# Reciprocal roots of a layer norm on GpSimd, two token tiles at a time, and normalising spread among later work

## The chip, the cores and the metric

The kernel runs on one core of a Trainium2 chip. A core has a matrix engine (TensorE, "PE" in the profile, with its weight loads as "PEld"), a vector engine (VectorE, "DVE"), a scalar engine (ScalarE, "ACT"), a general engine (GpSimd, "POOL") and an engine that issues transfers (SyncE, "SP"). Each runs its own instructions in order; between engines, semaphores say when data is ready. The metric is the device time of one execution in microseconds.

## The reference

Two stages follow each other. The first is attention with a sliding window of 128 positions and 4 sink positions, for 4 batches, 8 heads, 768 positions and 64 values a head. The second is a gated MLP over the 512 joined values of a position:

```python
h = gelu(x @ w_in)                      # 512 -> 1024
u, v = h[..., :512], h[..., 512:]
mu  = mean(v, axis=-1); var = mean((v - mu) ** 2, axis=-1)
v_n = (v - mu) / sqrt(var + 1e-06) * g_ln
v_s = einsum('ts,bsd->btd', w_sg, v_n) + b_sg[None, :, None]
out = x + (u * v_s) @ w_out
```

The mean and the variance are taken per position over 512 values. The product with w_sg mixes all 768 positions, so its first result needs the normalised values of every position of the batch.

## The kernel before, in words

The order of the instructions is written out by hand (manual_schedule): each engine does its work in the order in which the Python code issues it.

Attention runs over 16 pairs of heads (four pairs a batch). For a pair n, GpSimd casts q and k to bf16 (repack, issued two pairs ahead), TensorE transposes them, computes scores (score), ScalarE takes exponentials, VectorE multiplies by the band mask (keep_band), and TensorE multiplies by v (values); VectorE then divides by the sum of the row (L315, L316) and so writes x. GpSimd also copies the four sink keys (L214) and issues the loads of v and of the weights; SP issues the loads of q and k, the transposes of x and the output stores.

The MLP of a batch b, called a block here, is worked on when the first pair of the next batch has its scores (n = 4, 8, 12), and once more after the last pair. The function hidden(b, between) issues it:

- hidden_v for each of six token tiles j of 128 positions: four matmuls into PSUM (hv), Gelu on ScalarE into v_all (L335), bn_stats (L337) and bn_aggr (L338) on VectorE, which leave mean and variance in mv. After tiles 0 and 1 some of the values steps of the next batch are put in between (the list "between").
- hidden_u eight times: four matmuls (hu) and Gelu into uT (L348).
- inverse_root, issued after the first hidden_u: VectorE computes the reciprocal root of all six variances of a position at once, on tiles of 128x6: it adds 1e-6 (L357), makes a first guess by an integer shift and a subtraction on the bits (L358, L360), and takes three Newton steps of three instructions each (L364, L366, L367). That is 12 instructions.
- normalise, six times, one after each of the next hidden_u: VectorE subtracts the mean and multiplies by the reciprocal root, v_all to vn, 128x512 (L373).

What follows is put into a list of fillers: spatial (six matmuls over the six token tiles of vn, L383, then two VectorE instructions, L386 and L389, of which the first reads b_bc and g_sb) eight times, and project (L397) six times. For batch 0 the list begins with six transposes of w_sg (spatial_weights: wps on TensorE, wsgT on VectorE, L182). The main loop spreads the fillers among the attention steps of the next batch; for the last block there is no attention left, and they run one after the other. The tag "mm" in PSUM, which hv, hu, wps, vs and o_ps share, has two buffers.

Of the kernel before, what the change touches and what calls it, by code (L numbers as in the profile page):

```python
# [8 lines left out]
F32 = mybir.dt.float32  # L9
BF16 = mybir.dt.bfloat16  # L10
AF = mybir.ActivationFunctionType
ALU = mybir.AluOpType
# [5 lines left out]
def kernel(  # L18
# [14 lines left out]
    nc = tc.nc  # L33
# [7 lines left out]
    NT = S // 128  # L41
# [11 lines left out]
    small = ctx.enter_context(tc.tile_pool(name="small", bufs=4))  # L53
# [123 lines left out]
    def spatial_weights(si):  # L177
        wps = ps_m.tile([128, NT, 128], BF16, name="wps", tag="mm")
        for ti in range(NT):
            nc.tensor.transpose(wps[:, ti, :],  # L180
                                wsg_sb[:, ti, 128 * si:128 * (si + 1)], iden)
        nc.vector.tensor_copy(wsgT[:, si, :], wps.rearrange("p t q -> p (t q)"))  # L182
# [142 lines left out]
    uTs, vns, gTs, v_alls, mvs, rstds = {}, {}, {}, {}, {}, {}  # L325

    def hidden_v(b, j):
        if j == 0:
            v_alls[b] = work.tile([128, NT, DF], F32, name="v_all", tag="v_all", bufs=1)
            mvs[b] = small.tile([128, NT, 2], F32, name="mv", bufs=2)  # L330
        h_ps = ps_m.tile([128, 512], F32, name="hv", tag="mm")
        for c in range(KD):
            nc.tensor.matmul(h_ps, xT[b][:, c, 128 * j:128 * (j + 1)],  # L333
                             w_in_sb[:, c, DF:], start=(c == 0), stop=(c == KD - 1))
        nc.scalar.activation(out=v_alls[b][:, j, :], in_=h_ps, func=AF.Gelu_apprx_tanh)  # L335
        st = small.tile([128, 6], F32, name="st")
        nc.vector.bn_stats(out=st, in_=v_alls[b][:, j, :])  # L337
        nc.vector.bn_aggr(out=mvs[b][:, j, :], in_=st)  # L338

    def hidden_u(b, f, n):  # L340
        if f == 0 and n == 0:
            uTs[b] = work.tile([128, KU, S], BF16, name="uT")
        h_ps = ps_m.tile([128, 512], F32, name="hu", tag="mm")
        for c in range(KD):
            nc.tensor.matmul(h_ps[:, 0:NH], w_in_sb[:, c, 128 * f:128 * (f + 1)],  # L345
                             xT[b][:, c, NH * n:NH * (n + 1)],
                             start=(c == 0), stop=(c == KD - 1))
        nc.scalar.activation(out=uTs[b][:, f, NH * n:NH * (n + 1)],  # L348
                             in_=h_ps[:, 0:NH], func=AF.Gelu_apprx_tanh)

    I32 = mybir.dt.int32

    def inverse_root(b):
        rstd = rstds[b] = small.tile([128, NT], F32, name="rstd", bufs=2)
        var = small.tile([128, NT], F32, name="var", bufs=2)
        tmp = small.tile([128, NT], F32, name="tmp", bufs=2)
        nc.vector.tensor_scalar_add(var, mvs[b][:, :, 1], 1e-6)  # L357
        nc.vector.tensor_single_scalar(tmp.bitcast(I32), var.bitcast(I32), 1,  # L358
                                       op=ALU.logical_shift_right)
        nc.vector.tensor_scalar(out=rstd.bitcast(I32), in0=tmp.bitcast(I32),  # L360
                                scalar1=-1.0, scalar2=float(0x5F3759DF),
                                op0=ALU.mult, op1=ALU.add)
        for _ in range(3):
            nc.vector.scalar_tensor_tensor(out=tmp, in0=rstd, scalar=-0.5, in1=rstd,  # L364
                                           op0=ALU.mult, op1=ALU.mult)
            nc.vector.tensor_mul(tmp, tmp, var)  # L366
            nc.vector.scalar_tensor_tensor(out=rstd, in0=tmp, scalar=1.5, in1=rstd,  # L367
                                           op0=ALU.add, op1=ALU.mult)

    def normalise(b, j):  # L370
        if j == 0:
            vns[b] = work.tile([128, NT, DF], BF16, name="vn")
        nc.vector.tensor_scalar(out=vns[b][:, j, :], in0=v_alls[b][:, j, :],  # L373
                                scalar1=mvs[b][:, j, 0:1], scalar2=rstds[b][:, j:j + 1],
                                op0=ALU.subtract, op1=ALU.mult)

    def spatial(b, f, n):
        if f == 0 and n == 0:
            gTs[b] = work.tile([128, KU, S], BF16, name="gT")
        cols = slice(NH * n, NH * (n + 1))  # L380
        vs = ps_m.tile([128, 512], F32, name="vs", tag="mm")
        for si in range(NT):
            nc.tensor.matmul(vs[:, 0:NH], vns[b][:, si, 128 * f:128 * (f + 1)],  # L383
                             wsgT[:, si, cols], start=(si == 0), stop=(si == NT - 1))
        gv = small.tile([128, NH], BF16, name="gv")
        nc.vector.scalar_tensor_tensor(  # L386
            out=gv, in0=vs[:, 0:NH], scalar=g_sb[:, f:f + 1], in1=b_bc[:, cols],
            op0=ALU.mult, op1=ALU.add)
        nc.vector.tensor_mul(gTs[b][:, f, cols], gv, uTs[b][:, f, cols])  # L389

    def project(b, t, queue=nc.sync, by=nc.vector, cols=slice(0, DM)):
        rows = slice(128 * t, 128 * (t + 1))
        o_ps = ps_m.tile([128, 512], F32, name="o_ps", tag="mm")[:, 0:cols.stop - cols.start]
        whole = by is nc.vector
        res = x_sb[b][:, cols.start // 128:cols.stop // 128, t, :]
        for c in range(KU):
            nc.tensor.matmul(o_ps, gTs[b][:, c, rows], w_out_sb[:, c, cols],  # L397
                             start=(c == 0), stop=(c == KU - 1 and whole))
        if whole:
            o_sb = small.tile([128, DM], F32, name="o_sb", bufs=6)  # L400
            nc.vector.tensor_add(  # L401
                o_sb[:, cols].rearrange("p (h d) -> p h d", d=128),
                o_ps.rearrange("p (h d) -> p h d", d=128), res)
        else:
            nc.tensor.matmul(o_ps.rearrange("p (h d) -> p h d", d=128), iden, res,
                             start=False, stop=True)
            o_sb = small.tile([128, DM], F32, name="o_act", bufs=3)
            nc.scalar.copy(o_sb[:, cols], o_ps)
        queue.dma_start(out=out[b, rows, cols], in_=o_sb[:, cols])

    def project_halves(b, t, queue):
        project(b, t, queue, nc.scalar, slice(DM // 2, DM))
        project(b, t, queue, nc.vector, slice(0, DM // 2))
# [8 lines left out]
    def hidden(b, between, queue=nc.sync):  # L422
        def step():
            if between:
                between.pop(0)()

        for j in range(NT):
            hidden_v(b, j)
            for _ in range(min(j + 1, 2)):
                step()  # L430
        for i in range(2 * KU):
            hidden_u(b, i % KU, i // KU)
            if i == 0:
                inverse_root(b)
            elif i <= NT:
                normalise(b, i - 1)
        if b == 0 and queue is nc.sync:
            fillers.extend(lambda si=si: spatial_weights(si) for si in range(NT))
        for n in range(2):
            for f in range(KU):  # L440
                fillers.append(lambda f=f, n=n: spatial(b, f, n))
        for t in range(NT):
            if b == B - 1 and t == NT - 1:
                fillers.append(lambda t=t: project_halves(b, t, queue))
            else:
                by = nc.scalar if b == B - 2 else nc.vector
                fillers.append(lambda t=t, by=by: project(b, t, queue, by))
# [104 lines left out]
    def stable_path():  # L552
        keep, push = stable_masks()
        for b in range(B):
            for hp in range(HP):
                stable_pair(HP * b + hp, keep, push)
            hidden(b, [], nc.gpsimd)
            fill(len(fillers))
# [12 lines left out]
    for n in range(NP):  # L571
# [44 lines left out]
        if n % HP == 0 and n > 0:  # L616
            fill(len(fillers))
            hidden(n // HP - 1, [lambda i=i: values(n, i) for i in range(HT)])
            half_valued = n
# [10 lines left out]
    compare_inverses()  # L630
    fill(1)
    hidden(B - 1, [])
    fill(2)
    for eng in (nc.tensor, nc.vector, nc.scalar, nc.gpsimd):
# [43 lines left out]
```

## Time and profile before

| | |
|---|---|
| median of 3 runs | 180.08 us (179.92 to 180.32) |
| the profiled execution | 180.66 us |
| its span, first to last instruction | 178.80 us |
| busy: TensorE / VectorE / ScalarE / GpSimd | 156.6 / 146.0 / 119.4 / 57.5 us |
| L373 normalise, 24 instructions | 11.3 us, 543 ns each |
| L364, L366, L367 Newton steps, 12 instructions each | 2.0 us each line, 166 ns each |
| GpSimd, 128x768 cast of q or k (L191) | 823 ns (k), 826 ns (q, median) |
| GpSimd, 64x4 copy of the sink keys (L214) | 185 ns median, 180 to 376 |

How to read it: the profile is one execution. A line of a group names the source line, the engine, the operation, the tiles written and read and the number of instructions; after the bar stand the busy time in us, the mean duration in ns, and the idle time of the engine just before those instructions with what ended it. A line of a timeline has the start in us from the beginning of the span, the duration in us, the engine, the line and the tiles, and in brackets the idle time ahead of it; equal instructions that follow each other are drawn together (x6). The "chain that ended last" follows the execution back from its last instruction, at each step to what released it.

### The profile page before, as it was taken

The numbers are of one execution on the slowest core, as the hardware profiler recorded it, in microseconds if no ns is written. First come the engines' busy times: TensorE is split into PE (matmuls) and PEld (weight loads), VectorE is DVE, ScalarE is ACT, GpSimd is POOL, SyncE is SP. The second block draws the span as 40 slices with busy tenths as digits, with TensorE's granted clock in tenths as the row PEclk, the third lists the DMA queues.
The fourth block names the chain that finished last, engine by engine and source line by source line (L and its number), as shares of the span: only waits on it lengthen the run. The fifth ranks groups of instructions, "written<-read, shape, count | busy, mean of one in ns | idle before, by whom it ended". The sixth has DMA issues, their size and how long they took to land.

```text
span 178.8 us, 3744 instructions
## 1 busy us (share of the span) xinstructions
PE 156.6 (88%) x1407; PEld 88.7 (50%) x1418; DVE 146.0 (82%) x359; ACT 119.4 (67%) x168; POOL 57.5 (32%) x98
## 2 busy tenths in 40 slices
PE   0769779799689999899899999899799999999970
PEld 0447556345556555445456545355465554555430
DVE  5665989599889999698999998699999948858950
ACT  2488999867938668666968668877986856640000
POOL 8459999950042060425006070550010000000000
PEclk9999999999999999999999999999999999999999
DMA  5999999999857739895285969986202241011072
GB/s 158 266 306 265 267 271 273 191 207 218 103 179 48 202 66 209 303 270 39 20 219 33 214 183 192 380 108 44 44 4 44 50 178 59 0 63 60 0 294 66
DMA packets 47974, 27.24 MB, mean 152 GB/s; under 512 B 33680, under 2 KB 44944, under 8 KB 47952
## 3 DMA queue, kind: packets, MB, share of 16 engines
q0 software_dynamic: 27904, 6.31, 37.5%
q1 hardware_dynamic: 19504, 20.26, 37.5%
q10 hardware_dynamic: 544, 0.39, 0.7%
q8 instruction: 12, 0.20, 0.5%
q14 instruction: 10, 0.08, 0.1%
HBM read 24.81 MB, written 6.29 MB: 174 GB/s over the span
## 4 chain that ended last, share of the span: by engine, by line
PE 75%; ACT 12%; issue 4%; DVE 4%; DMA 2%
PE vs L383 17%; PE hu L345 13%; PE o_ps L397 11%; PE hv L333 11%; ACT ex L264 7%; PE sc L260 7%; PE cps L197 5%; PE av L305 4%; ACT kT L204 3%; PE scs L275 2%; PE av L308 2%; DMA k_sb<-in_k_dram 2%; ACT qT L204 2%; PE av L311 1%; DVE ex L271 1%
## 5 line engine op out<-in xcount | busy, mean ns | idle before, releaser
L264 ACT ACTIVATE ex<-sc 128x1024 bf16<-128x1024 f32 (+1 forms) x48 | 45.6, 958 | 16.9 <-PE sc L260 16.7
L383 PE MATMUL vs<-wsgT,vn 128*128 128x384 bf16 x192 | 35.5, 327 | 0.5 <-DVE wsgT L182 0.4
L191 POOL CAST k_bf<-k_sb 128x768 bf16<-128x768 f32 x15 | 12.3, 823 | 42.7 <-DMA k_sb<-in_k_dram 31.8
L397 PE MATMUL o_ps<-w_out_sb,gT 128*128 128x512 bf16 (+1 forms) x93 | 23.8, 370 | 1.2 <-DVE o_sb L401 0.8
L271 DVE TENSOR_TENSOR ex<-ex,mask 128x1024 bf16<-128x1024 bf16 x32 | 23.0, 722 | 1.8 <-ACT ex L264 1.7
L333 PE MATMUL hv<-w_in_sb,xT 128*128 128x512 bf16 x92 | 22.2, 379 | 1.9 <-DVE xT L286 1.7
L383 PEld LDWEIGHTS <-vn 128*128 128x128 bf16 x192 | 17.9, 98 | 12.0 <-issue 1.2
L345 PE MATMUL hu<-xT,w_in_sb 128*128 128x384 bf16 x128 | 23.2, 325 | 0.1
L260 PE MATMUL sc<-qT,kT 64*128 64x256 bf16 x192 | 19.0, 280 | 2.2 <-DVE qT L240 1.3
L386 DVE SCALAR_TENSOR_TENSOR gv<-vs,g_sb,b_bc 128x384 bf16<-128x384 f32 x32 | 19.5, 611 | 1.7 <-PE vs L383 1.7
L348 ACT ACTIVATE uT<-hu 128x384 bf16<-128x384 f32 x32 | 15.7, 490 | 6.5 <-PE hu L345 6.3
L337 DVE BATCH_NORM_STATS2 st<-v_all 128x6 f32<-128x512 f32 x24 | 16.3, 677 | 4.6 <-ACT v_all L335 4.5
L335 ACT ACTIVATE v_all<-hv 128x512 f32<-128x512 f32 x24 | 14.3, 597 | 7.2 <-PE hv L333 6.9
L316 DVE TENSOR_TENSOR x<-av,inverses 128x384 bf16<-128x384 f32 x32 | 17.8, 557 | 1.1
L305 PE MATMUL av<-v_sb,ex 128*128 128x65 bf16 x192 | 18.2, 198 | 0.2 <-DVE x L316 0.2
L305 PEld LDWEIGHTS <-ex 128*128 128x128 bf16 x192 | 14.5, 100 | 7.2 <-issue 2.9
L345 PEld LDWEIGHTS <-w_in_sb 128*128 128x128 bf16 x128 | 12.4, 97 | 10.7 <-issue 2.9
L87 POOL DMA_DIRECT2D v_sb<-in_v_dram x16 | 16.6, 1036 | 0.0
L308 PE MATMUL av<-v_sb,ex 128*128 128x65 bf16 x160 | 16.5, 197 | 0.0
L214 POOL COPY sk<-kT 64x4 bf16<-64x4 bf16 x30 | 6.2, 207 | 28.2 <-ACT kT L204 27.3
L191 POOL CAST q_bf<-q_sb 128x768 bf16<-128x768 f32 x15 | 14.1, 938 | 3.0 <-DMA q_sb<-in_q_dram 2.2
L333 PEld LDWEIGHTS <-xT 128*128 128x128 bf16 x96 | 9.0, 98 | 11.9 <-DVE xT L286 2.6
(83 smaller groups left out, 241.4 us busy)
## 6 DMA issues: line engine op xcount, KB each, us to landing
k_sb<-in_k_dram SPq DMA_DIRECT2D x15, 384.0 KB, 5.5
q_sb<-in_q_dram SPq DMA_DIRECT2D x15, 384.0 KB, 6.1
out_dram<-o_sb SPq DMA_DIRECT2D x17, 256.0 KB, 3.5
v_sb<-in_v_dram POOLq DMA_DIRECT2D x16, 192.0 KB, 6.9
out_dram<-o_act SPq DMA_DIRECT2D x6, 256.0 KB, 2.0
wsg_sb<-in_moe_w_sg_dram POOLq DMA_DIRECT2D x2, 576.0 KB, 10.2
w_in_sb<-in_moe_w_in_dram POOLq DMA_DIRECT2D x4, 256.0 KB, 8.9
w_out_sb<-in_moe_w_out_dram POOLq DMA_DIRECT2D x1, 512.0 KB, 11.8
```

Of the source, the lines that this page charges most:

```text
L191: eng.tensor_copy(flat.rearrange("p t (h d) -> p h t d", h=2), src)
L260: nc.tensor.matmul(sc[:, hl, w:w + n_q], kT[rows, 128 * j:128 * (j + 1)], qT[rows, 128 * j:128 * j + n_q], start=True, stop=True)
L264: nc.scalar.activation(out=part, in_=sc[:, :, 0:w], func=AF.Exp, scale=scale)
L271: nc.vector.tensor_mul(part, part, m)
L305: nc.tensor.matmul(av[:, m, hl, :], probs(i, hl, 0), v_sb[:, hl, i, :], start=(m == 0 and hl == 0), stop=False)
L308: nc.tensor.matmul(av[:, m, hl, :], probs(i - 1, hl, 1), v_sb[:, hl, i - 1, :], start=False, stop=False)
L316: nc.vector.tensor_mul(x_sb[b][:, hp, HT * c:HT * (c + 1), :].rearrange("p i (h d) -> p i h d", h=2), av[:, :, :, 0:64], rcp.to_broadcast( ...
L333: nc.tensor.matmul(h_ps, xT[b][:, c, 128 * j:128 * (j + 1)], w_in_sb[:, c, DF:], start=(c == 0), stop=(c == KD - 1))
L345: nc.tensor.matmul(h_ps[:, 0:NH], w_in_sb[:, c, 128 * f:128 * (f + 1)], xT[b][:, c, NH * n:NH * (n + 1)], start=(c == 0), stop=(c == KD - 1))
L383: nc.tensor.matmul(vs[:, 0:NH], vns[b][:, si, 128 * f:128 * (f + 1)], wsgT[:, si, cols], start=(si == 0), stop=(si == NT - 1))
L386: nc.vector.scalar_tensor_tensor(out=gv, in0=vs[:, 0:NH], scalar=g_sb[:, f:f + 1], in1=b_bc[:, cols], op0=ALU.mult, op1=ALU.add)
L397: nc.tensor.matmul(o_ps, gTs[b][:, c, rows], w_out_sb[:, c, cols], start=(c == 0), stop=(c == KU - 1 and whole))
```

## The change

The reciprocal roots are made by GpSimd instead of VectorE, in three groups of two token tiles (128x2), each issued as soon as the statistics of its two tiles are issued. The seed no longer needs a shift: one instruction multiplies the bits as an integer by -0.5 and adds the constant. A Newton step is four GpSimd instructions instead of three on VectorE, so a group has 14 instructions. The normalising of tile 0 is issued after the statistics of tile 3, that of tile 1 after those of tile 4, that of tile 2 after those of tile 5, and the other three after the first three hidden_u. The tiles var and tmp have four buffers instead of two.

```diff
-    def inverse_root(b):
-        rstd = rstds[b] = small.tile([128, NT], F32, name="rstd", bufs=2)
-        var = small.tile([128, NT], F32, name="var", bufs=2)
-        tmp = small.tile([128, NT], F32, name="tmp", bufs=2)
-        nc.vector.tensor_scalar_add(var, mvs[b][:, :, 1], 1e-6)
-        nc.vector.tensor_single_scalar(tmp.bitcast(I32), var.bitcast(I32), 1,
-                                       op=ALU.logical_shift_right)
-        nc.vector.tensor_scalar(out=rstd.bitcast(I32), in0=tmp.bitcast(I32),
-                                scalar1=-1.0, scalar2=float(0x5F3759DF),
+    def inverse_root(b, j):
+        if j == 0:
+            rstds[b] = small.tile([128, NT], F32, name="rstd", bufs=2)
+        rstd = rstds[b][:, j:j + 2]
+        var = small.tile([128, 2], F32, name="var")
+        tmp = small.tile([128, 2], F32, name="tmp")
+        nc.gpsimd.tensor_scalar_add(var, mvs[b][:, j:j + 2, 1], 1e-6)
+        nc.gpsimd.tensor_scalar(out=rstd.bitcast(I32), in0=var.bitcast(I32),
+                                scalar1=-0.5, scalar2=float(0x5F3759DF),
                                 op0=ALU.mult, op1=ALU.add)
         for _ in range(3):
-            nc.vector.scalar_tensor_tensor(out=tmp, in0=rstd, scalar=-0.5, in1=rstd,
-                                           op0=ALU.mult, op1=ALU.mult)
-            nc.vector.tensor_mul(tmp, tmp, var)
-            nc.vector.scalar_tensor_tensor(out=rstd, in0=tmp, scalar=1.5, in1=rstd,
-                                           op0=ALU.add, op1=ALU.mult)
+            nc.gpsimd.tensor_mul(tmp, rstd, rstd)
+            nc.gpsimd.tensor_mul(tmp, tmp, var)
+            nc.gpsimd.tensor_scalar(out=tmp, in0=tmp, scalar1=-0.5, scalar2=1.5,
+                                    op0=ALU.mult, op1=ALU.add)
+            nc.gpsimd.tensor_mul(rstd, tmp, rstd)
...
         for j in range(NT):
             hidden_v(b, j)
+            if j % 2 == 1:
+                inverse_root(b, j - 1)
             for _ in range(min(j + 1, 2)):
                 step()
+            if j >= 3:
+                normalise(b, j - 3)
         for i in range(2 * KU):
             hidden_u(b, i % KU, i // KU)
-            if i == 0:
-                inverse_root(b)
-            elif i <= NT:
-                normalise(b, i - 1)
+            if i < NT - 3:
+                normalise(b, i + 3)
```

In the compiled order of GpSimd the 42 instructions of block 0 stand ahead of the casts of pair 7, of its v load and of the loads of b_bc, g_sb and w_out; those of blocks 1 and 2 stand ahead of the casts and the v load of pairs 11 and 15. Each of the 42 waits for the one before it.

## The prediction

> **What bounds the kernel now.** I first read the page's chain that ended last, then the groups, then the instructions of VectorE in time order around the edited code.
>
> ```profile
> PE 156.6 (88%) x1407; PEld 88.7 (50%) x1418; DVE 146.0 (82%) x359; ACT 119.4 (67%) x168; POOL 57.5 (32%) x98
> PE 75%; ACT 12%; issue 4%; DVE 4%; DMA 2%
> L383 PE MATMUL vs<-wsgT,vn 128*128 128x384 bf16 x192 | 35.5, 327 | 0.5 <-DVE wsgT L182 0.4
> L383 PEld LDWEIGHTS <-vn 128*128 128x128 bf16 x192 | 17.9, 98 | 12.0 <-issue 1.2 <-DVE vn L373 0.9
> ```
>
> TensorE carries 75% of the chain, VectorE 4%. The edited code feeds TensorE through vn alone, and TensorE's weight loads waited 0.9 us for it in all. So at most about that can be won directly at vn; what can be lost is whatever vn becomes late by. In the last block nothing else is left for TensorE to do, and its row of VectorE shows how late vn may be:
>
> ```profile
> 148.74 0.69 DVE L337 BATCH_NORM_STATS2 st<-v_all 128x6 f32<-128x512 f32 x1
> 149.47 0.18 DVE L338 BATCH_NORM_AGGREGATE mv<-st 128x2 f32<-128x6 f32 x1
> ...
> 152.92 0.18 DVE L338 BATCH_NORM_AGGREGATE mv<-st 128x2 f32<-128x6 f32 x1
> 153.14 0.17 DVE L357 TENSOR_SCALAR var<-mv 128x6 f32<-128x6 f32 x1
> 153.34 0.17 DVE L358 TENSOR_SCALAR tmp<-var 128x6 int32<-128x6 int32 x1
> ...
> 155.56 2.83 DVE L373 TENSOR_SCALAR vn<-v_all,mv,rstd 128x512 bf16<-128x512 f32 x6
> ```
>
> ```profile
> 159.37 7.97 PE L383 MATMUL vs<-wsgT,vn 128*128 128x384 bf16 x48
> ```
>
> vn is complete at 158.39 and the spatial products begin at 159.37; the sixth of them, the first to need the last token tile, starts 5 x 0.165 later at 160.2. Slack: 1.8 us. Two rows price GpSimd and its sharing with VectorE:
>
> ```profile
> 5.46 0.42 POOL L244 COPY sk<-kT 64x4 bf16<-64x4 bf16 x2 [0.78 <-ACT kT L238]
> ```
>
> ```profile
> 82.05 1.01 POOL L87 DMA_DIRECT2D v_sb<-in_v_dram  x1
> ```
>
> ```profile
> 82.38 0.66 DVE L360 TENSOR_SCALAR rstd<-tmp 128x6 int32<-128x6 int32 x1
> ```
>
> The pair of tiny copies, the second of which waits for the first, takes 0.42 us at 0.18 each: a dependent step is 0.24. And L360, 0.17 us when alone, lasted 0.66 and ended at 83.04 with the GpSimd instruction beside it (83.06).
>
> **The change, part by part.**
>
> *Removed from VectorE:* 12 instructions a block, from 153.14 to 155.56, 2.4 us, four times. Off TensorE's path except through vn, so worth nothing unless vn comes earlier.
>
> *Added on GpSimd:* three groups of 14 dependent instructions a block (one add, one seed, three times four), 42 steps in a row. Price p of a step: from above the 128x128 affine selects on GpSimd (0.29) plus the 0.06 hand-over seen in the pair, 0.35; from below the 128x1 memset (0.10, reads nothing) plus 0.06, 0.16. The nearest row is the tiny copy, 0.24, but nine of the fourteen read two operands, so I go a quarter of the way up: p = 0.27, a group 3.8 us, three groups 11.3 us. They cannot overlap: GpSimd runs in order and each starts where the one before ended.
>
> *The wait that this adds:* normalise of tile 0 now stands on VectorE behind the statistics of tile 3 and waits for group 0; behind it are queued the statistics of tiles 4 and 5, on which group 2 depends. Walk for the last block: statistics of tile 1 end at 149.65, group 0 runs 149.75 to 153.5; normalise 0, statistics 4, normalise 1, statistics 5 (0.47, 0.8, 0.47, 0.8) end at 156.1, inside group 1; tiles 2 and 3 follow group 1, tiles 4 and 5 group 2, another 1.0.
>
> *Contention:* the four normalisings beside groups 1 and 2 and GpSimd's instructions hold each other up, as L360 shows. Bounds per normalising: 0, and its whole 0.54. I take 0.4 (its pace, 2.83/6 = 0.47, less the hand-over gap), C = 1.6 us a block (0 to 2.2). [...]
>
> So vn is complete S + 42p + C + 1.0 = S + 13.9 us, where S is 0.1 after the statistics of tile 1. Each block has a time D up to which that costs nothing:
>
> - Block 0: S = 36.0, so 49.9. VectorE's next work came at 45.01 with 0.77 idle behind it, D = 45.8: reciprocal, mask multiplies and the six wsgT copies all lie behind normalise, and TensorE's first spatial product waited for a wsgT copy. +4.1.
> - Block 1: S = 77.75, 91.7. vn ended at 87.71 with TensorE already waiting; only the 0.67 that it then idled for the kT copy absorbs anything, D = 88.4. +3.3.
> - Block 2: S = 116.1, 130.0. vn 125.71 plus an idle 0.93, D = 126.6. +3.4.
> - Block 3: S = 149.75, 163.7, D = 160.1. +3.6, nothing behind it to hide in.
>
> Sum 14.4 us. After blocks 0 to 2 TensorE is the chain again, so I take nothing back.
>
> *What GpSimd queues behind the groups:* casts of a later pair, its v load, the sk copies. In block 1 the casts of pair 11 move from 80.3 to about 90, and TensorE transposes them from 93.7 (then also later): covered. In block 2 the casts of pair 15 move from 117.4 to about 128.5 against 131.2: covered, with 1 us to spare and TensorE late as well. SP's loads into the freed buffers were waiting behind the transposes and output stores on SP's queue anyway (long waits of L321 and L409 there), so they do not move by this. In block 0 more is queued: casts and v load of pair 7, then b_bc, g_sb and w_out, issued at 36.0 to 38.1 before. Group 2 ends at 48.9; casts 1.8 and v load 1.04 put b_bc at 51.7. It took 10.6 us to land then, behind two 576 KB loads in the same queue; the k_sb loads of the same 384 KB take 5.2 (median). By 5.2 it lands at 57, g_sb a little later; gv, now due at 56.2, must end before the third spatial unit at 58.3 (two PSUM buffers). I take +1.0 (0 to 4.7).
>
> *Moved on VectorE:* six normalisings, the same count and form, costed in the walk.
>
> Total +15.4. The profiled execution took 180.66 us (span 178.80), the median of the runs is 180.08; 180.66 + 15.4 = 196.1, against the median **195.5 us**.
>
> **Rivals.**
>
> 1. *The step is dear where two operands are read.* Nine at 0.35 and five at 0.24 make a group 4.35 us: delays of 5.8, 5.0, 5.2 and 5.3, with b_bc 22.3, **202.4 us**; all at 0.35, +29, **209 us**. For it: nothing in the trace shows GpSimd with two inputs. Against: these are two elements a partition, and the affine selects' 0.29 has 128 in it. [...]
> 2. *b_bc lands late in block 0:* at 10.6 us gv ends at 63.0, TensorE loses 4.7 instead of 1.0, **199 us**. For: the only row of that load. Against: the large loads ahead of it are gone by then.
> 3. *No contention and the copy's 0.24:* delays of 1.2, 0.4, 0.5 and 0.7, **183 us**. For: the gaps between GpSimd's steps may be enough for a normalising. Against: L360.
> 4. *The other side: the groups finish in time and VectorE gains.* Place: the deadlines D above; D minus S is 9.8 to 10.6, so with C = 1.6 it decides at p = 0.17 to 0.19. With p = 0.16 and C = 0, vn is complete 7.7 after S, 0.9 to 2.3 us sooner than before, and the waits for vn (0.9) and wsgT (0.8) go: 180.08 - 1.7 = **178.4 us**; with C = 1.6 it ends near 180. For: memsets of 0.10. Against: they read nothing, and every GpSimd instruction that reads SBUF here lasts at least 0.18.
>
> **How the numbers follow.** Forecast (p 0.22 to 0.31, 186 to 203): 0.62. Rival 1: 0.14. Rival 2: 0.06. Rival 3: 0.08. Rival 4: 0.10, of it 0.06 faster and 0.04 no difference (0.2% is about what a measurement of this kernel can tell). Faster 0.06, same 0.04, slower 0.90. The range goes from rival 3 to the upper end of rival 1: 183.5 to 209; the forecast's own is 186 to 203.
>
> **What the changed profile would show.** L373 no longer six in a row but with VectorE idle before tiles 0, 2 and 4, released by GpSimd's rstd (by the walk about 2.1, 2.0 and 3.7 us in the last block). GpSimd's groups 3.8 us long, back to back, longer where a normalising lies in them. TensorE's weight load at L383 waiting for vn three to five us in each of blocks 1 to 3 and for wsgT in block 0. What makes me wrong: steps under 0.19 us, or GpSimd starting a dependent step without the 0.06 hand-over.

## The result, and the profile after

The changed kernel took **202.1 us** (median of 4 runs, 201.2 to 204.0) against 180.2 us for the kernel before on the same chip (179.9 to 180.7). The ratio is **1.120**, 95% interval 1.115 to 1.125: 12% slower. The profiled execution took 201.21 us with a span of 199.4, against 180.66 and 178.8, so the two profiles differ by 20.6 us of span. The forecast was 195.5 us with a range of 183.5 to 209. The direction and the range held; 6.6 us were missing. Each ratio below is to the kernel before on the same chip and leaves out executions more than 1.5% above the fastest of their kernel; the profiled executions of experiment 1, of the kernel with two Newton steps (5) and of the early loads alone (7) are such slow ones.

The page of the changed kernel: the busy line and the row of TensorE's granted clock (PEclk, in tenths, 40 equal slices), the chain that ended last, and the groups around the edit.

```profile
PE 164.1 (82%) x1407; PEld 90.7 (45%) x1418; DVE 140.4 (70%) x311; ACT 119.4 (60%) x168; POOL 93.6 (47%) x266
PEclk9999999999589999999789999998599999996996
PE 36%; POOL 26%; DVE 12%; issue 10%; DMA 9%; ACT 4%; ACTq 0%; POOLq 0%; DVEq 0%
L383 PE MATMUL vs<-wsgT,vn 128*128 128x384 bf16 x192 | 41.1, 355 | 11.2 <-DVE vn L373 10.6
L373 DVE TENSOR_SCALAR vn<-v_all,mv,rstd 128x512 bf16<-128x512 f32 x24 | 15.2, 660 | 26.6 <-POOL rstd L368 26.6
L383 PEld LDWEIGHTS <-vn 128*128 128x128 bf16 x192 | 19.1, 105 | 26.9 <-DVE vn L373 13.1
```

GpSimd has gone into the chain with 26%, TensorE has fallen from 75% to 36%. (Most of the 9% of DMA are loads at the start of the kernel, up to 12.9 us, and the load of g_sb in block 0.) VectorE stands idle for 26.6 us in front of its normalisings (0.1 before), TensorE's matmuls and weight loads stand idle behind vn. And the clock row is no longer all nines: there is a dip in each block (the last slice lies at the end of the work). The 192 spatial matmuls are the same, but take 355 ns each instead of 327.

The last block, GpSimd in time order (start, duration, engine and line; the idle time ahead in brackets):

```profile
165.88 0.21 POOL L359 TENSOR_SCALAR var<-mv 128x2 f32<-128x2 f32 x1 [16.81 <-DVE mv L338]
166.18 0.19 POOL L360 TENSOR_SCALAR rstd<-var 128x2 int32<-128x2 int32 x1
166.45 0.19 POOL L364 TENSOR_TENSOR tmp<-rstd 128x2 f32<-128x2 f32 x1
166.72 0.20 POOL L365 TENSOR_TENSOR tmp<-tmp,var 128x2 f32<-128x2 f32 x1
167.00 0.19 POOL L366 TENSOR_SCALAR tmp<-tmp 128x2 f32<-128x2 f32 x1
...
169.76 0.21 POOL L359 TENSOR_SCALAR var<-mv 128x2 f32<-128x2 f32 x1
...
173.84 0.21 POOL L359 TENSOR_SCALAR var<-mv 128x2 f32<-128x2 f32 x1
...
174.47 0.38 POOL L364 TENSOR_TENSOR tmp<-rstd 128x2 f32<-128x2 f32 x1
```

A step lasts 0.19 to 0.21 and the next one starts 0.27 to 0.30 after it starts, whether it reads one operand or two. The first group takes 3.88 us (165.88 to 169.76), the second 4.08; in it and in the third a few steps are longer, 0.38 at most, where a normalising runs on VectorE. VectorE and TensorE in the same block:

```profile
169.71 0.55 DVE L373 TENSOR_SCALAR vn<-v_all,mv,rstd 128x512 bf16<-128x512 f32 x1 [2.27 <-POOL rstd L368]
...
173.79 1.00 DVE L373 TENSOR_SCALAR vn<-v_all,mv,rstd 128x512 bf16<-128x512 f32 x2 [1.47 <-POOL rstd L368]
177.92 1.00 DVE L373 TENSOR_SCALAR vn<-v_all,mv,rstd 128x512 bf16<-128x512 f32 x2 [3.12 <-POOL rstd L368]
```

```profile
175.44 0.82 PE L383 MATMUL vs<-wsgT,vn 128*128 128x384 bf16 x4
178.52 5.72 PE L383 MATMUL vs<-wsgT,vn 128*128 128x384 bf16 x22 [2.25 <-DVE vn L373]
```

VectorE waits before tiles 0, 2 and 4, as the walk said. vn is complete at 178.92. TensorE does four products with the tiles that are there, then stands for 2.25 us. Twenty-two products in 5.72 us are 0.26 each; before the change 48 took 7.97, 0.166 each. Most of that is the clock. These are windows of the changed kernel: for three of its slow stretches the 3.4 us ahead, then the stretch. The columns are the busy time of each engine with the number of instructions, then the granted clock (PEclk), the share of the DMA engines and GB/s:

```profile
175.84:179.24 3.40, 1.03 (x6) 0.34 (x5) 1.06 (x3) 0.24 (x1) 1.46 (x8) 1.00 0.41 154
179.24:182.68 3.44, 3.44 (x13) 1.60 (x12) 1.96 (x4) 0.00 (x0) 0.00 (x0) 0.50 0.01 2
93.94:97.35 3.41, 0.69 (x4) 0.28 (x6) 2.35 (x4) 0.21 (x1) 3.16 (x7) 1.00 0.01 2
97.35:100.76 3.41, 3.41 (x20) 1.51 (x19) 2.58 (x6) 1.71 (x2) 1.10 (x3) 0.50 1.16 108
134.90:138.30 3.40, 1.12 (x8) 0.25 (x4) 0.96 (x2) 2.36 (x3) 2.50 (x12) 1.00 0.00 0
138.30:145.10 6.80, 4.60 (x23) 1.85 (x24) 5.13 (x9) 1.71 (x2) 3.98 (x8) 0.50 0.62 51
```

TensorE was busy for 1.03, 0.69 and 1.12 us of 3.4 at the full clock (30%, 20% and 33%); then the granted clock is 0.50 for 3.4 us, or twice that. The wait for vn is thus paid twice: while it lasts, and in the work right behind it, where six spatial products take 2.12 us (at 98.38, block 1) instead of 1.14.

The profiles of all the runs together say more. In each of them the changes of the granted clock lie multiples of 3.41 us apart (in the changed kernel's it halves at 49.55, 97.34, 138.30 and 179.26 us and is whole again at 56.38, 100.75, 145.13 and 182.67). Cut into windows at these marks, the 14 profiles have 29 windows at full clock in which TensorE's matmuls were busy for 45% or less, and half clock follows every one of them; it follows none of the 625 windows above 57%, and 5 of the 17 between. At half clock, windows of 78% or less were followed by half clock again, those of 88% or more by full clock. So in these profiles half clock goes with the share of a window in which TensorE works, and the change lies between 45% and 57%. The marks lie at other times in each profile (in block 0 half clock begins at 49.55 us in the changed kernel's, at 51.4 in the one-group kernel's of experiment 2). In the kernel with two Newton steps (experiment 5) TensorE was busy for 1.33 us of the 3.41 from 46.69 us on, 39%, and yet the twelve spatial products behind it took 2.11 us, their time at full clock. So it seems to matter how a wait lies to the marks, which no run shows by itself.

Where the 20.6 us lie, from the first matmul of one block's hv to the next block's (the fourth: to the end of the span; us):

| | block 0 | block 1 | block 2 | block 3 |
|---|---|---|---|---|
| before | 43.09 | 37.56 | 34.51 | 32.63 |
| after | 48.66 | 42.42 | 40.61 | 37.16 |
| longer by | 5.57 | 4.86 | 6.10 | 4.53 |
| predicted | 5.1 (4.1 and 1.0) | 3.3 | 3.4 | 3.6 |

The first stage starts 0.46 us earlier in this execution, which is the rest. So the delays came in the right blocks, and those of blocks 1 to 3 were sized 0.9 to 2.7 us too small in the forecast. The experiments ask what that remainder is, and which part of the change costs the rest.

### The profile page after: what moved, and what is told of

It is laid out like the page before. It is cut to its first block, busy times and chain, and to the rows that moved or that the text cites. A ratio compares the mean times of both kernels' runs of the same rounds, so it can differ in the third digit from the quotient of the medians.

```text
span 199.4 us, 3868 instructions
## 1 busy us (share of the span) xinstructions
PE 164.1 (82%) x1407; PEld 90.7 (45%) x1418; DVE 140.4 (70%) x311; ACT 119.4 (60%) x168; POOL 93.6 (47%) x266
## 4 chain that ended last, share of the span: by engine, by line
PE 36%; POOL 26%; DVE 12%; issue 10%; DMA 9%; ACT 4%; ACTq 0%; POOLq 0%; DVEq 0%
PE vs L383 12%; PE o_ps L397 9%; DMA q_sb<-in_q_dram 6%; PE sc L260 4%; POOL tmp L364 4%; POOL rstd L368 4%; POOL tmp L365 4%; POOL tmp L366 4%; DMA g_sb<-in_moe_g_ln_dram 3%; PE cps L197 3%; DVE gv L386 3%; DVE vn L373 2%; PE av L305 2%; POOL q_bf L191 2%; PE hv L333 2%
## 5 line engine op out<-in xcount | busy, mean ns | idle before, releaser
L383 PE MATMUL vs<-wsgT,vn 128*128 128x384 bf16 x192 | 41.1, 355 | 11.2 <-DVE vn L373 10.6
L373 DVE TENSOR_SCALAR vn<-v_all,mv,rstd 128x512 bf16<-128x512 f32 x24 | 15.2, 660 | 26.6 <-POOL rstd L368 26.6
L383 PEld LDWEIGHTS <-vn 128*128 128x128 bf16 x192 | 19.1, 105 | 26.9 <-DVE vn L373 13.1
L191 POOL CAST k_bf<-k_sb 128x768 bf16<-128x768 f32 x15 | 13.4, 896 | 37.8 <-DMA k_sb<-in_k_dram 33.3
L271 DVE TENSOR_TENSOR ex<-ex,mask 128x1024 bf16<-128x1024 bf16 x32 | 23.6, 739 | 0.7 <-ACT ex L264 0.7
L260 PE MATMUL sc<-qT,kT 64*128 64x256 bf16 x192 | 19.6, 289 | 2.2 <-DVE qT L240 1.3
L337 DVE BATCH_NORM_STATS2 st<-v_all 128x6 f32<-128x512 f32 x24 | 16.4, 683 | 4.6 <-ACT v_all L335 4.5
L305 PE MATMUL av<-v_sb,ex 128*128 128x65 bf16 x192 | 17.8, 196 | 0.5 <-DVE x L316 0.5
L308 PE MATMUL av<-v_sb,ex 128*128 128x65 bf16 x160 | 16.1, 195 | 0.0
L408 ACT COPY o_act<-o_ps 128x512 f32<-128x512 f32 (+1 forms) x7 | 3.7, 549 | 20.3 <-PE o_ps L405 20.3
L191 POOL CAST q_bf<-q_sb 128x768 bf16<-128x768 f32 x15 | 13.5, 899 | 5.0 <-DMA q_sb<-in_q_dram 3.2
```

Source lines behind the costliest of these rows:

```text
L191: eng.tensor_copy(flat.rearrange("p t (h d) -> p h t d", h=2), src)
L260: nc.tensor.matmul(sc[:, hl, w:w + n_q], kT[rows, 128 * j:128 * (j + 1)], qT[rows, 128 * j:128 * j + n_q], start=True, stop=True)
L271: nc.vector.tensor_mul(part, part, m)
L305: nc.tensor.matmul(av[:, m, hl, :], probs(i, hl, 0), v_sb[:, hl, i, :], start=(m == 0 and hl == 0), stop=False)
```

## The experiments

**1. Is the clock a cost of its own?** The changed kernel, with matmuls that nobody reads where TensorE would wait: ahead of the third transposes of w_sg in block 0, and ahead of the first spatial products in blocks 1 to 3.

```diff
+    def keep_busy(ps, count):
+        for _ in range(count):
+            nc.tensor.matmul(ps, w_in_sb[:, 0, 0:128], w_in_sb[:, 0, 0:384],
+                             start=True, stop=True)
     def spatial_weights(si):
+        if si == 2:
+            keep_busy(ps_t.tile([128, 384], F32, name="busy", tag="tp"), 18)
...
+        if b > 0 and f == 0 and n == 0:
+            keep_busy(vs[:, 0:NH], 14 if b == B - 1 else 22)
```

> The changed kernel with idle matmuls put where TensorE waits (18 between the second and the third transposition of w_sg in block 0, 22 ahead of the first spatial product in blocks 1 and 2, 14 in block 3; each overwritten or never read). GpSimd and VectorE are untouched. Theory A (the waits for vn cost about 15 us, and the rest of the 22 us is TensorE's granted clock, which reads 0.5 for some microseconds after each long wait): the clock stays near 1.00 and the time falls to 196 us (194 to 199). Theory B (the half clock lies beside other engines' work and costs nothing; the waits alone make the 22 us): 201 to 203 us, whatever the clock reads.

Measured: 197.73 us (196.9 to 199.9), ratio 1.0944 [1.0892, 1.0997]. The idle matmuls made the kernel 4.4 us faster than without them (ratio 1.094 instead of 1.120). In the profiled execution (199.9 us, the slowest of the four) block 1 went from 42.42 to 41.18 and the last from 37.16 to 35.64; block 2 still had a stretch at half clock (143.0 to 146.4) and was longer (41.65 against 40.61), as its group 0 started 2.2 us after the statistics of tile 1 (0.95 without the idle matmuls); block 0 was no shorter (48.83), and VectorE waited there 1.90 us for g_sb (1.53 in the changed kernel):

```profile
57.15 0.62 DVE L395 SCALAR_TENSOR_TENSOR gv<-vs,g_sb,b_bc 128x384 bf16<-128x384 f32 x1 [1.90 <-DMA g_sb<-in_moe_g_ln_dram]
```

Theory A held: with the clock at 0.982 to 0.998 instead of 0.934 to 0.948 the time is inside its 194 to 199. The clock is a term that the forecast did not have.

**2. Is it the engine or the three groups?** Two kernels undo one half of the change each. The first keeps GpSimd, but takes all six variances at once, with the normalisings where they were before:

```diff
-            if j % 2 == 1:
-                inverse_root(b, j - 1)
-            if j >= 3:
-                normalise(b, j - 3)
...
-            if i < NT - 3:
-                normalise(b, i + 3)
+            if i == 0:
+                inverse_root(b)
+            elif i <= NT:
+                normalise(b, i - 1)
```

> Only the engine is changed: GpSimd computes all six roots in one group of 14 steps, at the place of before, and the normalising stays where it was. Theory A (what counts is the number of dependent steps in a row, 0.275 us each on GpSimd): one group takes 3.9 us against 2.4 us on VectorE, vn comes 1.5 us later, of which 0.7 to 1.8 us is covered in each block: 182 us (181 to 184), no stretch of half clock. Theory B (GpSimd itself is at fault, by sharing with VectorE and by what its queue holds back): the casts and loads behind the group and the shared access stay, 190 us or more.

The second keeps the three groups and the spread normalisings, but makes the roots on VectorE, with the 12 instructions of before on 128x2:

> Only the grouping is changed: VectorE computes the roots in three groups of two tiles, 12 instructions each, and the normalising is spread as in the changed kernel. Theory A (three groups in a row triple a chain that does not get shorter with fewer columns): 36 instructions of 0.2 us are 7.3 us instead of 2.4, all on VectorE between the statistics, vn is complete some 4 us later than before in each block, and the time is 198 us (193 to 203), with half clock after the waits. Theory B (GpSimd's slow steps are the cause and groups are harmless): 180 to 185 us.

Measured: one group on GpSimd 188.70 us, ratio 1.046 [1.0424, 1.0496]; three groups on VectorE 202.43 us, ratio 1.1208 [1.1157, 1.1259], which is the changed kernel's own ratio. So the larger part is the cutting into three: the chain of short dependent steps is run three times in a row, on either engine. (Cutting and spreading the normalisings go together in both kernels; that the spreading costs nothing by itself is seen in experiment 5, where a kernel with both and one Newton step loses nothing.) In the last block of the VectorE version:

```profile
167.83 0.17 DVE L359 TENSOR_SCALAR var<-mv 128x2 f32<-128x2 f32 x1
...
170.00 0.16 DVE L369 SCALAR_TENSOR_TENSOR rstd<-tmp,rstd 128x2 f32<-128x2 f32 x1
170.08 0.69 DVE L337 BATCH_NORM_STATS2 st<-v_all 128x6 f32<-128x512 f32 x1
```

A group of 12 takes 2.3 us there for two columns, and in the kernel before it takes 2.4 for six: with so few columns the price is per instruction, not per element. Three times 2.3 also hold up the statistics, which stand behind them on VectorE. Theory A's 193 to 203 held, at its upper end.

For the single group both theories missed, 182 and 190 or more against 188.7. Theory A's group length was right, 39.94 to 43.83. Its "no stretch of half clock" was not: there are two, 51.4 to 54.8 and 133.3 to 136.7 us. What else it lacked was in VectorE's rows and GpSimd's, each of the one-group kernel:

```profile
43.87 4.55 DVE L371 TENSOR_SCALAR vn<-v_all,mv,rstd 128x512 bf16<-128x512 f32 x6 [4.11 <-POOL rstd L366]
```

```profile
43.77 0.82 POOL L191 CAST k_bf<-k_sb 128x768 bf16<-128x768 f32 x1
44.55 1.02 POOL L191 CAST q_bf<-q_sb 128x768 bf16<-128x768 f32 x1
45.51 1.11 POOL L87 DMA_DIRECT2D v_sb<-in_v_dram  x1
```

Six normalisings took 4.55 us instead of 2.83. GpSimd's casts had waited behind the group, and so they start just when the normalisings do: the first three of the six last 1.02 to 1.08 us, the others 0.53 to 0.75. The three slow normalisings end 0.2 to 0.3 us after the GpSimd instruction beside them, and in block 3, where no casts follow, all six take 0.54 to 0.55. Why the two engines hold each other up, no run shows.

**3. Are the casts to blame?** The one-group kernel with the casts and the v load of pairs 7, 11 and 15 issued behind the keys of the next pair:

```diff
-        if n + 2 < NP:
+        behind = n > HP and n % HP == 1
+        if n + 2 < NP and not behind:
             repack(n + 2, G)
             load_v(n + 2)
...
+            if g == 0 and behind:
+                repack(n + 2, G)
+                load_v(n + 2)
```

> The kernel with one group on GpSimd (188.7 us), with the casts and the v load of pairs 7, 11 and 15 put behind the copies of the sink keys, which wait for a copy by ScalarE, so that GpSimd is idle while VectorE normalises. Theory A (the six normalisings took 4.55 us instead of 2.83 because GpSimd's casts ran beside them, 1.7 us in each of three blocks): the six take 2.83 again and the time falls by 4 to 6 us, to 183 to 185 us. Theory B (the normalisings beside the casts lie on no path, the longer chain of roots makes the whole loss): 188 to 189 us.

Measured: 187.07 us, ratio 1.0337 [1.0298, 1.0375], between the two theories. The six normalisings were back at 2.83 us in block 1:

```profile
89.63 2.83 DVE L371 TENSOR_SCALAR vn<-v_all,mv,rstd 128x512 bf16<-128x512 f32 x6 [4.08 <-POOL rstd L366]
```

In block 0 they took 3.35. But the casts then lay beside the mask multiplies (1.15 and 1.31 us instead of 0.68), so that 1.6 us were won where A expected 3.7 to 5.7. By blocks of the two profiled executions, block 1 lasts 39.01 us in both; the gain lies in block 2 (37.62 to 35.65), where the one-group kernel has a stretch at half clock and this one has none. So moving the casts only moved their price, and that they cost the one-group kernel its 1.7 us a block is not shown. And block 0 (46.96 us against 43.09) had a stretch at half clock, 50.4 to 57.2:

```profile
52.00:54.00 2.00, 2.00 (x12) 1.20 (x11) 1.22 (x3) 0.59 (x1) 0.00 (x0) 0.50 1.10 321
54.00:56.00 2.00, 2.00 (x8) 0.92 (x7) 0.88 (x2) 0.00 (x0) 1.28 (x2) 0.50 1.86 208
```

**4. What was that stretch worth?** Ten idle matmuls more, in block 0 (the expectation says "in each block", but the transposes of w_sg, ahead of the third of which they stand, are issued in block 0 alone):

```diff
     def spatial_weights(si):
+        if si == 2:
+            keep_busy(ps_t.tile([128, 384], F32, name="busy", tag="tp"), 10)
```

> The kernel of one group of 14 GpSimd steps with the casts of pairs 7, 11 and 15 put later, plus ten matmuls of 384 columns into a spare PSUM tile ahead of the third of the spatial units' four parts in each block, so that TensorE stays at work through the stretch in which it is only about a third busy. Theory A: of what that kernel (187.07 us) is over the kernel before, about 2 us is the half clock of block 0 (twelve matmuls took 4.04 us instead of 2.11); with TensorE kept busy the clock stays whole, block 0 is 45.0 us instead of 46.96, and the time is 185 (184 to 186). Theory B: the half clock only filled time that TensorE would have waited anyway, and the matmuls change nothing or cost their own time: 187 to 188.

Measured: 186.14 us, ratio 1.0287 [1.0206, 1.0368]. Its granted clock stayed 1.00 throughout the block, and the first twelve spatial products took 2.11 us instead of 4.04:

```profile
53.91 2.11 PE L388 MATMUL vs<-wsgT,vn 128*128 128x384 bf16 x12 [0.75 <-DVE wsgT L189]
```

But block 0 was 46.35 us, only 0.6 shorter, since the idle matmuls themselves (1.79 us) put the first product from 52.92 to 53.91. Neither theory met the size: the half clock was gone, but half of its price was paid to be rid of it. A gain from idle matmuls is therefore rather too low than too high for what the clock costs.

**5. How much hangs on the number of steps?** The changed kernel with two Newton steps instead of three (the diff), then with one. These compute less exact roots: they leave part of the computation out.

```diff
-        for _ in range(3):
+        for _ in range(2):
```

> The changed kernel with two Newton steps instead of three (the third is left out), 10 instructions a group. Theory A (a race against the time by which vn is needed): 12 steps fewer bring vn 3.3 us earlier in each block, which is about what it is late by, so nearly the whole loss goes at once, the half clock with it: 182 us (180 to 185). Theory B (the loss is in proportion to GpSimd's work): ten fourteenths of 22 us stay, 196 us.

> The changed kernel with one Newton step (two are left out), 6 instructions a group, 18 in a row or 5 us a block. Theory A (a race against the time by which vn is needed): the last group now waits for the last statistics instead of the group before it, vn is in time in every block but for the casts beside its last two tiles: 180 us (178.5 to 182), clock near 1.00. Theory B (sharing and waiting on GpSimd cost by themselves, however few steps): 184 us or more, not much below the kernel with two steps (184.0).

Measured: 183.99 us with two steps, ratio 1.0186 [1.0141, 1.0231]; 180.72 us with one, ratio 1.001 [0.9983, 1.0036]. The first four instructions out of a group of 14 are worth 18 us, the next four 3 us. Twelve steps fewer a block are 3.3 us by the step of 0.275, 13 us in four blocks. The other 5 are about what experiments 1 and 8 give for the clock, whose mean is 0.983 to 0.999 in the executions with two steps (0.934 to 0.948 in the changed kernel); that they are the clock's is argued from these means, not shown by a run. Theory A held in both kernels. With one step a group lasts 1.67 us, and of the last block's waits for rstd one is left:

```profile
154.88 0.97 DVE L373 TENSOR_SCALAR vn<-v_all,mv,rstd 128x512 bf16<-128x512 f32 x2
157.04 1.00 DVE L373 TENSOR_SCALAR vn<-v_all,mv,rstd 128x512 bf16<-128x512 f32 x2 [1.19 <-POOL rstd L368]
```

vn is complete at 158.04, before TensorE asks for it at 160.28. Even so the kernel is no faster than before. Its profiled execution has a stretch at half clock in block 0 (49.2 to 52.7 us) although vn is complete there as early as before; but the three executions with a mean clock of 0.999 or more took 180.4 to 180.5 us, so that stretch hides no gain.

**6. What the idea gives with few steps and the casts moved.** Two Newton steps, a group of four tiles and one of two, the normalisings where they were before, the casts later as in 3, and b_bc, g_sb and w_out loaded one pair sooner:

```diff
-            if j % 2 == 1:
-                inverse_root(b, j - 1)
+            if j == NT - 3:
+                inverse_root(b, 0, NT - 2)
+            if j == NT - 1:
+                inverse_root(b, NT - 2)
...
-        load_weights(n)
+        if n != 5:
+            load_weights(n)
+        if n == 4:
+            load_weights(5)
```

> An attempt to be faster than both: two Newton steps, GpSimd in two groups (four tiles behind the statistics of tile 3, two behind those of tile 5), the normalising behind the hidden_u as before, b_bc, g_sb and w_out issued ahead of the groups, and the casts of pairs 7, 11 and 15 behind the sink copies. Theory A (20 steps of 0.275 us end 0.9 us before VectorE's own roots did, and VectorE has 2.4 us a block less to do): vn is never waited for, 179 us (178.4 to 180.2). Theory B (any GpSimd work beside the statistics and the normalising costs what it saves): 181 us or more.

Measured: 182.41 us, ratio 1.0114 [1.0079, 1.0149]. Theory B's 181 or more held. As theory A said, vn is in time (TensorE waits 0.2 us for it in all), the normalisings run at their full pace (0.55 at most), and block 0 is 43.17 us, as before the change (43.09). Most of what the profiled execution (181.73 us) loses lies in blocks 1 and 2 (37.93 and 35.28 against 37.56 and 34.51), where VectorE's row shows the casts again, now beside the gating and the masks:

```profile
89.40 0.99 DVE L389 TENSOR_TENSOR gT<-gv,uT 128x384 bf16<-128x384 bf16 x1
90.31 1.30 DVE L271 TENSOR_TENSOR ex<-ex,mask 128x1024 bf16<-128x1024 bf16 x1
```

Against 0.36 and 0.69 alone, that is 1.2 us.

**7. The wait for g_sb.** The changed kernel with b_bc, g_sb and w_out loaded one pair sooner (the last four lines of the diff in 6), without idle matmuls and with those of experiment 1:

> The changed kernel with the loads of b_bc, g_sb and w_out issued at pair 4, ahead of the groups of block 0, instead of behind them. Theory A (the wait of 1.53 us for g_sb in block 0 is on the path): 200.5 us, 1 to 2 us below the changed kernel. Theory B (covered by the two PSUM buffers): no change, 202 us.

> The changed kernel with the idle matmuls that keep TensorE's clock up, and with b_bc, g_sb and w_out loaded one pair sooner, so that their descriptors stand ahead of the groups in GpSimd's queue. Theory A: with the clock kept, block 0 is bound by g_sb (VectorE waited 1.90 us for it), so that the early loads take 1.5 to 2 us from block 0 (48.8 to about 47) and the time is 196 (195 to 196.8). Theory B: behind the late load the late roots stand ready as the next wait, as they did in the kernel with the early loads alone: 197.3 to 198.2.

Measured: 202.41 us without, ratio 1.120 [1.1167, 1.1233], no change. In the changed kernel VectorE had waited 1.53 us for g_sb at 57.17; with the early load that wait is gone, and it waits 1.38 for TensorE in its place, which has been at half clock from 53.6 to 60.5. Theory B's 202 held; behind the late load the late roots and the half clock were ready as the next limit. With the idle matmuls the four executions spread from 195.4 to 202.2 us, so the median (199.2) is no verdict. In the profiled one block 0 is 47.52 against 48.83, and the wait for g_sb is gone:

```profile
56.15 0.62 DVE L395 SCALAR_TENSOR_TENSOR gv<-vs,g_sb,b_bc 128x384 bf16<-128x384 f32 x1 [0.76 <-PE vs L392]
```

That points to theory A and 1.3 us; one execution of each kernel is not enough to show it.

**8. The clock kept in all four blocks.** The second kernel of experiment 7 with 38 idle matmuls instead of 22 in block 2, the last that dipped:

```diff
-            keep_busy(vs[:, 0:NH], 14 if b == B - 1 else 22)
+            keep_busy(vs[:, 0:NH], (0, 22, 38, 14)[b])
```

> The kernel before this one (idle matmuls and early loads), with 38 idle matmuls instead of 22 in block 2, whose stretch at half clock was the last one left in its profile (TensorE idle 1.65 us after the 22, then 139.2 to 142.4 us at 0.50). Theory A: the clock is then whole in all four blocks, block 2 goes from 41.1 us to about 39.3, and what is left over the kernel before the change is lateness of the roots alone: the one execution that kept a clock of 0.999 took 195.4 us, so 195 (194 to 196.3). Theory B: the half clock of block 2 was filled by waiting, as most of that of block 0 was in the kernel with one group, and the time stays at 196.8 to 199.5.

Measured: 197.53 us (196.3 to 198.9), ratio 1.0949 [1.0887, 1.1011]. In the profile the clock is whole, here the windows that held the slow stretch of block 2:

```profile
138.00:140.00 2.00, 2.00 (x15) 1.03 (x15) 1.97 (x4) 0.00 (x0) 2.00 (x3) 1.00 0.00 0
140.00:142.00 2.00, 2.00 (x22) 1.05 (x22) 1.97 (x5) 1.59 (x2) 0.95 (x3) 1.00 1.05 68
```

The stages are 47.91, 40.90, 39.64 and 36.07. Block 2 went from 41.12 to 39.64, as theory A said, but the total stayed at B's 196.8 to 199.5: it is the same as experiment 1's 197.73 within the scatter of these kernels. What the longer idle run wins in one block is not seen in the median.

**9. Was there anything to win?** The kernel before, roots on VectorE as they were, with two Newton steps; again less exact.

```diff
-        for _ in range(3):
+        for _ in range(2):
```

> The kernel before with two Newton steps instead of three, on VectorE as before (the roots are then less exact). It asks what the chain of short steps costs where it stood before the change: three instructions fewer in each block. Theory A: the chain lies on the path of the end, as the roots are the last thing before the block's normalisings: 4 x 3 steps of a tenth to a fifth of a us are 1 to 2 us less, 178 to 179.2. Theory B: it lay beside TensorE's own chain, which the roots did not hold up: 179.8 to 180.3, no change.

Measured: 180.63 us, ratio 1.0005 [0.9973, 1.0038]. The chain is 0.6 us shorter in each block, and nothing is faster. Theory B's "no change" held (the time lies above its 179.8 to 180.3, but so does that of the kernel before on this chip, 180.68): the roots before the change lay beside TensorE's own work.

## Why the prediction was right, and where it was not

*What bounds the kernel* was right: TensorE, with vn's lateness as the only way in. The 0.9 us of waits for vn said that little could be won, and experiments 5 and 9 agree: neither roots of one Newton step on GpSimd, which bring vn earlier, nor a chain on VectorE that is 0.6 us shorter made the kernel faster.

*The price of a step* was right: 0.27 forecast, 0.275 measured from start to start, a group 3.88 us against 3.8. The bounds of 0.16 and 0.35 were far from it on either side. The quarter of the way up that was added for a second operand turned out to be the hand-over, which was nearer 0.085 than 0.06.

*The walk* was right in its order. VectorE's waits in the last block were 2.27, 1.47 and 3.12 us where 2.1, 2.0 and 3.7 were named.

*The contention* had about the right size in the wrong place, which is luck. It was put on groups 1 and 2, 1.6 us a block; there it was 0.4 (two groups of 4.08 instead of 3.88). But the last two normalisings, which the sum took at 1.0, took 1.97 in blocks 0 to 2, where the casts of a later pair run right behind group 2, and 1.00 in block 3, where there are none. Block 1 of the changed kernel, VectorE's row and GpSimd's:

```profile
94.96 1.97 DVE L373 TENSOR_SCALAR vn<-v_all,mv,rstd 128x512 bf16<-128x512 f32 x2 [3.12 <-POOL rstd L368]
```

```profile
94.87 0.82 POOL L191 CAST k_bf<-k_sb 128x768 bf16<-128x768 f32 x1
95.63 1.02 POOL L191 CAST q_bf<-q_sb 128x768 bf16<-128x768 f32 x1
```

The step that failed is "covered", said of those casts: what waits for them was covered, but what they run beside was not looked at. Experiments 2, 3 and 6 show it from three sides: wherever the casts were put behind the statistics, they slowed the work of VectorE beside them.

From the end of the statistics of tile 1 plus 0.1 to vn complete, the sum said 13.9 us; the trace has 14.1, 14.1, 14.9 and 13.1 for blocks 0 to 3. The near agreement of blocks 0 and 1 comes of two errors that cancel: 1.2 too much in the groups' contention, 1.0 too little for the last two normalisings, and 0.3 in the sum of the steps. The 14.9 has a row of its own: in block 2 group 0 could not start at 126.1, since GpSimd was still at the descriptors of a v load and the sk copies, and began at 126.94. "S is 0.1 after the statistics of tile 1" did not ask what stood in GpSimd's queue *ahead* of the group; in the profile before, the sk copies of block 2 (116.25, 0.44 us) end at 116.69, 0.6 behind the 116.1 that was taken for S.

*The missing term is the granted clock.* "After blocks 0 to 2 TensorE is the chain again, so I take nothing back" took TensorE's work behind the wait at its old duration. It ran at half clock for 3.4 to 6.8 us in blocks 1 to 3, and from 49.6 to 56.4 us in block 0. With idle matmuls the kernel is 4.4 us faster (202.1 to 197.7 us), by experiment 4 rather less than that price. With the clock whole in all blocks and the loads early (experiment 8), what is left over the kernel before is 4.8, 3.3, 5.1 and 3.4 us by blocks, against 4.1, 3.3, 3.4 and 3.6 predicted without the 1.0 for the loads. The lateness was sized well but for block 2, whose group 0 started 1.5 us late in that profile. The change takes 20.6 us of span more than the kernel before and experiment 8's kernel 16.4; these 4.2 us are the clock and the early loads together, and the early loads alone took nothing (experiment 7).

*b_bc and g_sb, +1.0:* a wait of 1.53 us was there at the place named, but with the half clock beside it, it cost nothing (experiment 7); with the clock kept it is worth 1.3 by one profile of each kernel, which does not show it.

*The rivals.* Rival 1 gives the nearest times, 202.4 and 209, but for the wrong reason: a step with two operands lasts 0.19 us (medians of 193 to 195 ns), as one with one operand does (191 ns, L366). Rival 2 (b_bc as late as 10.6 us after its issue) did not come: g_sb was issued at 50.93, and VectorE, which reads both, went on at 57.17. Rival 3 was nearly right about the contention in the groups (0.4 us, where it had none) and wrong about the step. Rival 4 fell: p was 0.275, where it needed 0.19 or less. Experiment 5's kernel with one Newton step (a group of 1.67 us) puts its condition to the test: vn is in time, and the time is that of before (ratio 1.001), not 178.4. There was no gain behind the condition.

What stays open: how the clock's 4.4 us or more divide over the blocks, since the idle matmuls both keep the clock and delay what follows; how much of the early loads' 1.3 us is real; and how the 8.3 us of the one-group kernel divide over the longer group, the casts and its two stretches at half clock.

## What to carry to other kernels

The chains of short dependent instructions took here what their count says, not their columns (14 steps on GpSimd 3.88 us for two columns and 3.89 for six, 12 on VectorE 2.3 and 2.4), so cutting the data into three tripled them on either engine; before moving such a chain, look whether anyone waits for it. In these profiles half clock, for 3.4 us or more, followed every window of 3.41 us at full clock in which TensorE was busy for 45% or less; where a change makes TensorE wait like that (here 2.25 to 4.14 us), price the work behind the wait at half clock on top of the wait. And for every instruction that slides behind the moved ones, ask not only who waits for it but what it will now run beside (beside the casts two normalisings took 1.97 us instead of 1.00).

## What the runs showed of the hardware that was not expected

- A 128x2 instruction on GpSimd lasts 0.19 us and the next dependent one starts 0.275 us after its start; TENSOR_TENSOR with two inputs (medians of 193 to 195 ns) is not dearer than TENSOR_SCALAR with one (191 ns, L366).
- The half clock came after a window of 3.4 us in which TensorE was busy for up to 1.12 us (changed kernel, 134.90 to 138.30). Over the 14 profiles it came after every window of 3.41 us with TensorE busy for 45% or less and after none above 57%; full clock came back after windows with 88% or more. In the one-group kernel with the casts moved it came with no wait of TensorE above 1.31 us from 44 to 51 us, when it was busy for 1.49 us of the 4 from 46 to 50.
- Beside GpSimd's 128x768 casts a mask multiply of 0.69 us took up to 1.31, a gating multiply of 0.36 took 0.99, and two normalisings of 1.00 took 1.97; beside GpSimd's 128x2 steps in the changed kernel a normalising kept its 0.55, and only single steps grew, from 0.19 to 0.38 at most.
